# Attention weights as pairs of 16-bit floats, turned by DMA; q and k loaded twice, one copy above the other

## The chip, the core and the metric

The kernel runs on one core of a Trainium2 chip. A core has five engines with queues of their own: TensorE (PE; its weight loads are listed apart as PEld), VectorE (DVE), ScalarE (ACT), GpSimd (POOL) and SyncE (SP), which here issues the DMAs. Each engine works through its own list of instructions in order and waits on semaphores for the others. The metric is the time of one execution in device microseconds; less is better.

## The reference

The kernel computes three layers after one another: block-causal attention, a mixture of experts with dense gates, and a two-layer network with a softmax-weighted activation and a normalization. The change is in the attention alone, cut here to what it computes:

```
B, H, S, D = 4, 8, 576, 64                        # q, k, v: [B, H, S, D] in f32
scores = (1/8) * q @ k^T                          # per (batch, head): 576 x 576
mask   = (row // 64) >= (column // 64)            # blocks of 64
attn   = softmax(where(mask, scores, -1e9))       # divided by (sum + 1e-9)
x      = attn @ v                                 # 2304 x 512 over all heads
...                                               # gates, 8 experts (512 -> 1024 -> 512), then w_in, w_out
```

## The kernel before

The 32 (batch, head) pairs are worked in 16 **head pairs**; the two heads of one are n and n+1. A head's 576 queries are cut into tiles of 128 queries, t = 0 to 3, and the last 64 queries of both heads together are the even head's tile t = 4. So a head pair is nine tiles, and `attention()` works 144 tiles as a software pipeline: in step k it calls `products` for tile k and the later stages for earlier tiles, by the depths in the table `steps` (`("turn", 3)` is tile k - 3).

For one tile the stages are these. `products` forms the scores on PE, in two passes over the split k (`kl`, `kh`) with a q tile that holds the high part in its upper 64 partitions and the low part in the lower 64; `maximum` and `invert` are small DVE operations around ACT's `exponent`, which writes `e` and its row sum. `weight` (L250, POOL) divides `e` by the sum in place. `turn` (L255, L258) transposes each 128 x 128 block of `e` on PE into PSUM. `place` (L278 on ACT, L279 on DVE) splits the turned block into a high and a low fp32r part: ACT copies the high part out of PSUM, DVE subtracts it from the PSUM block. `weigh` (L308, PE) multiplies with the split values `vs`, `sum` (L330, L331) adds the two halves of the result into `xr`, and `split` passes x on to the experts.

`prepare(n)` loads the next head pair: `kraw`, `qraw` and `vraw`, one DMA each, two heads above each other in the 128 partitions. POOL splits k (L64, L159) and v (L64, L184), ACT and DVE split q (L156, L160). `spread` then copies each head's 64 partitions to where the products need them, twice for k: 12 copies of 64 partitions from SBUF to SBUF for each head pair (L169 to L172), all issued on SP.

Into the same list of steps `fill(k)` weaves matmuls of the first expert (gates L405, layers L661 to L699) over the x that is ready; the table `fills` sets how much goes into which steps. The bulk starts at step k = 44. All tiles of PSUM in the attention, scores (`qk`), turned blocks (`tp`, `tq`) and results (`av`), come from one pool of six banks, `psp`. The order within each engine follows the program, moved in places by a scheduler. What comes behind the attention (the gates' normalization, the other experts, the last network) isn't touched.

## Time and profile before

| | |
|---|---|
| time, median of 3 runs | 1886.54 us (1886.08 to 1887.54) |
| the profiled execution | 1884.84 us, span 1883.1 us, granted clock 0.992 |
| PE busy | 1784.1 us (95%) |
| DVE busy | 1385.1 us (74%) |
| POOL busy | 1130.0 us (60%) |
| ACT busy | 852.5 us (45%) |
| DMA | 305.69 MB, mean 162 GB/s |

The span runs from the first to the last instruction; the profiled execution's own time has 1.7 us beside it. The attention with the expert work woven into it takes about the first 380 us. "Busy" is time in which an engine had an instruction of the program under way; the busy time of PE is modelled and counts overlapping matmuls once. The row of POOL's `weight` in the page's list of costly groups is 82.3 us for 144 instructions.

### The profile page before, as it was taken

The numbers are of one execution on the slowest core, as the hardware profiler recorded it, in microseconds if no ns is written. First come the engines' busy times: TensorE is split into PE (matmuls) and PEld (weight loads), VectorE is DVE, ScalarE is ACT, GpSimd is POOL, SyncE is SP. The second block draws the span as 40 slices with busy tenths as digits, with TensorE's granted clock in tenths as the row PEclk, the third lists the DMA queues.
The fourth block names the chain that finished last, engine by engine and source line by source line (L and its number), as shares of the span: only waits on it lengthen the run. The fifth ranks groups of instructions, "written<-read, shape, count | busy, mean of one in ns | idle before, by whom it ended". The sixth has DMA issues, their size and how long they took to land.

```text
span 1883.1 us, 30546 instructions
## 1 busy us (share of the span) xinstructions
PE 1784.1 (95%) x10234; PEld 1161.6 (62%) x10234; DVE 1385.1 (74%) x3199; ACT 852.5 (45%) x1737; POOL 1130.0 (60%) x962
## 2 busy tenths in 40 slices
PE   5799999979999999999999999999999999999999
PEld 4588998868444554554566555665565566566664
DVE  6878777765667666577687878778587898889873
ACT  5666766573777676753422222222322222225332
POOL 7665655345798868672566657668655656582110
PEclk8999999989999999999999999999999999999999
DMA  8665646253667556543656555556555455455433
GB/s 225 165 171 137 165 133 175 66 186 119 223 224 252 183 197 200 160 172 120 205 164 180 171 168 161 159 148 171 167 164 164 148 160 171 148 189 122 107 84 73
DMA packets 227678, 305.69 MB, mean 162 GB/s; under 512 B 57776, under 2 KB 113728, under 8 KB 225600
## 3 DMA queue, kind: packets, MB, share of 16 engines
q1 hardware_dynamic: 227520, 303.73, 54.2%
q8 instruction: 81, 1.33, 0.3%
q14 instruction: 77, 0.63, 0.1%
HBM read 190.86 MB, written 75.05 MB: 141 GB/s over the span
## 4 chain that ended last, share of the span: by engine, by line
PE 51%; POOL 14%; issue 14%; DVE 9%; DMA 5%; ACT 5%; SPq 2%; POOLq 0%; ACTq 0%; DVEq 0%
PE yps L842 4%; PE yps L844 4%; PE yps L843 4%; POOL hf L907 3%; POOL hb L910 3%; POOL w L567 2%; PE av L308 2%; POOL W L567 2%; PE psb L844 2%; PE psb L842 2%; PE psb L843 2%; PE ops L1316 2%; PE ops L1318 2%; PE ops L1317 2%; PE hps L661 1%
## 5 line engine op out<-in xcount | busy, mean ns | idle before, releaser
L907 POOL TENSOR_TENSOR hf<-hb,hf 128x768 f16<-128x768 f32 x196 | 322.3, 1665 | 202.2 <-ACT hf L906 198.6
L843 PEld LDWEIGHTS <-W 128*128 128x128 f16 x1960 | 191.6, 98 | 158.4 <-issue 33.0
L906 ACT CAST hf<-hb 128x768 f16<-128x768 f32 x196 | 155.9, 830 | 275.6 <-DVE hb L910 108.3
L842 PEld LDWEIGHTS <-W 128*128 128x128 f16 x1960 | 191.8, 98 | 135.2 <-ACT W L566 4.7
L844 PEld LDWEIGHTS <-W 128*128 128x128 f16 x1960 | 191.7, 98 | 128.1 <-POOL W L567 1.3
L842 PE MATMUL yps<-hf,W 128*128 128x384 f16 x784 | 255.1, 326 | 3.6 <-DVE acc L954 2.7
L843 PE MATMUL yps<-hf,W 128*128 128x384 f16 x784 | 255.6, 326 | 0.0
L844 PE MATMUL yps<-hf,W 128*128 128x384 f16 x784 | 254.8, 326 | 0.0
L954 DVE SCALAR_TENSOR_TENSOR acc<-yps,rscw,acc 128x384 f32<-128x384 f32 x364 | 215.9, 609 | 20.2 <-PE yps L844 19.1
L842 PE MATMUL psb<-X,W 128*128 128x384 f16 x504 | 164.2, 326 | 13.1 <-DVE u L854 7.5
L844 PE MATMUL psb<-X,W 128*128 128x384 f16 x504 | 164.0, 326 | 0.3 <-POOL W L567 0.3
L843 PE MATMUL psb<-X,W 128*128 128x384 f16 x504 | 164.3, 326 | 0.0
L910 POOL TENSOR_TENSOR hb<-hb 128x768 f32<-128x768 f32 x84 | 153.9, 1832 | 11.0 <-DVE hb L899 7.6
L854 DVE TENSOR_TENSOR u<-psb,r 128x384 f32<-128x384 f32 x168 | 91.3, 552 | 75.0 <-ACT r L868 36.5
L250 POOL TENSOR_SCALAR e<-e,sv 128x128 f32<-128x128 f32 (+2 forms) x144 | 82.3, 574 | 99.7 <-DVE sv L246 32.8
L1001 PE MATMUL yps<-w,h 128*128 128x512 f16 x336 | 127.3, 379 | 6.1 <-DVE h L888 3.3
L567 POOL TENSOR_TENSOR w<-raw,w 128x512 f16<-128x512 f32 (+1 forms) x96 | 122.0, 1289 | 10.8 <-ACT w L566 10.6
L1002 PE MATMUL yps<-w,h 128*128 128x512 f16 x336 | 127.3, 379 | 0.0
L1003 PE MATMUL yps<-w,h 128*128 128x512 f16 x336 | 127.0, 379 | 0.0
L842 PE MATMUL psc<-X,W 128*128 128x384 f16 x336 | 109.5, 326 | 5.7 <-DVE psa L854 2.8
L842 PE MATMUL psa<-X,W 128*128 128x384 f16 x336 | 109.5, 326 | 4.7 <-ACT r L868 4.6
L843 PE MATMUL psa<-X,W 128*128 128x384 f16 x336 | 109.5, 326 | 0.0
(266 smaller groups left out, 4473.4 us busy)
## 6 DMA issues: line engine op xcount, KB each, us to landing
W<-fd SPq DMA_DIRECT2D x392, 256.0 KB, 3.0
fd<-W SPq DMA_DIRECT2D x154, 256.0 KB, 2.1
raw<-in_w1s SPq DMA_DIRECT2D x14, 1024.0 KB, 6.1
raw<-in_w SPq DMA_DIRECT2D x14, 1024.0 KB, 7.5
fd<-w SPq DMA_DIRECT2D x84, 128.0 KB, 2.2
raw<-in_w SPq DMA_DIRECT2D x40, 256.0 KB, 3.3
kh<-khigh SPq DMA_DIRECT2D x64, 144.0 KB, 2.6
kl<-kraw SPq DMA_DIRECT2D x64, 144.0 KB, 2.7
```

What stands on the lines that cost most here:

```text
L567: nc.gpsimd.tensor_tensor(t[:, 1, :], raw, full(t[:, 0, :]), op=ALU.subtract)
L842: nc.tensor.matmul(ps, wh, xl, start=start and kc == 0, stop=False, skip_group_check=True)
L843: nc.tensor.matmul(ps, wh, xh, start=False, stop=False, skip_group_check=True)
L844: nc.tensor.matmul(ps, wl, xh, start=False, stop=stop and kc == 1, skip_group_check=True)
L854: nc.vector.tensor_tensor(to, bank[g, a], tmp[g, "r1" if a == "b" else name[1:]], op=ALU.add)
L906: nc.scalar.copy(hi, a)
L907: nc.gpsimd.tensor_tensor(lo, a, hi, op=ALU.subtract)
L910: eng.tensor_tensor(o, a, b, op=ALU.subtract)
L954: nc.vector.scalar_tensor_tensor(a, ps, r, a, op0=ALU.mult, op1=ALU.add)
L1001: nc.tensor.matmul(ps, hl, ws[c][:, 0, :], start=c == 0, stop=False)
L1002: nc.tensor.matmul(ps, hh, ws[c][:, 1, :], start=False, stop=False)
L1003: nc.tensor.matmul(ps, hh, ws[c][:, 0, :], start=False, stop=c == 3)
```

## The change

What it does, by parts (the line numbers here are those of the changed kernel):

- `weight`, the PE transposes of `turn` and `place` are gone. A new stage `halve`, at depth 2, has ACT write the high 16-bit half of `e` times the reciprocal sum (out of SBUF, `e` now has 640 columns with the last 64 zero), and DVE write the low half by a subtraction whose two tensors are both in SBUF (L284). The new `turn`, at depth 2 too, is a DMA transpose on SP from `eh` into the tiles `a1`, `a2` (L292; two of 64 partitions for tile t = 4, L296).
- The values are scaled by a power of two from their sum of squares and split into 16-bit halves; the scale is found by an ACT square (L192), a matmul with ones (L197) and five small DVE operations, and taken back out in `sum`. `weigh` multiplies 16-bit operands.
- q and k of each head are loaded from DRAM straight into both halves of the partitions, eight DMAs of 64 partitions and one of `vraw` for a head pair; `spread` is gone. k and q are split head by head, so each of these operations runs twice for a head pair.
- Depths: `weigh` from 5 to 6, `sum` from 6 to 7, `split` from 7 to 8. The `a1` and `a2` tiles have four buffers instead of two.

```
     def prepare(n):
...
+        for i in range(2):
+            kr, qr = krs.take(), qrs.take()
+            for r in (slice(0, D), slice(D, P)):
+                nc.sync.dma_start(kr[r], kT[b, h + i])
+            for r in (slice(0, D), slice(D, P)):
+                nc.sync.dma_start(qr[r], qT[b, h + i])
+            raws.append((kr, qr))
+            if i == 0:
+                nc.sync.dma_start(vraw, v[b, h // 2])
+                iv = ivs.take()
...
+        def high(i):
+            pool_copy(kh, kr)
+            nc.scalar.activation(q, qr, AF.Copy, scale=0.125)
+        def low(i):
+            nc.gpsimd.tensor_tensor(kl, kr, r32(kh), op=ALU.subtract)
+            nc.vector.scalar_tensor_tensor(
+                q[D:P], qr[D:P], 0.125, r32(q[D:P]), op0=ALU.mult, op1=ALU.subtract
+            )
...
+            nc.scalar.activation(vjunk, vraw, AF.Square, accum_out=r32(iv[:, 2:3]))
...
+            nc.tensor.matmul(ps[:, 0:1], ones, r32(iv[:, 2:3]), start=True, stop=True)
+            halved(iv[:, 0:1], ps[:, 0:1])
...
-        def spread(i):
-            for r in (slice(0, D), slice(D, P)):
-                nc.sync.dma_start(r32(kh[r]), r32(kh2[half]))
-                nc.sync.dma_start(r32(kl[r]), kraw[half])
-            nc.sync.dma_start(r32(q[0:D]), r32(qh2[half]))
-            nc.sync.dma_start(r32(q[D:P]), qraw[half])
...
-        def weight(self):
-            e = self.e[:, 0 : self.nk]
-            nc.gpsimd.tensor_scalar(e, e, self.rs, 1.0, op0=ALU.mult, op1=ALU.mult)
+        def halve(self):
+            k = self.k = self.t + 1
+            e = self.e[:, 0 : k * P].rearrange("p (k q) -> p k q", q=P)
+            eh = self.eh = ehs.take()
+            hi, lo = (eh[:, 0:k, s, :] for s in range(2))
+            nc.scalar.activation(hi, e, AF.Copy, scale=self.rs)
+            nc.vector.scalar_tensor_tensor(lo, e, self.rs, hi, op0=ALU.mult, op1=ALU.subtract)
 
         def turn(self):
-            self.tp = tp = psp.tile([P, 4, P], F32, tag="ps", name="tp")
-            for kt in range(min(self.t + 1, 4)):
-                nc.tensor.transpose(tp[:, kt, :], self.e[:, kt * P : kt * P + P], ident)
...
-        def place(self):
...
-            for dst, src in work:
-                nc.scalar.copy(dst(0), src)
-                nc.vector.tensor_tensor(dst(1), src, r32(dst(0)), op=ALU.subtract)
+            src = self.eh[:, 0 : self.k].rearrange("p k s q -> p (k s q)")
+            if t < 4:
+                a, c = (parts[n][0], t * P) if t < 2 else (parts[n][1], 64 + t * P - 256)
+                to = a.rearrange("p k s c -> p (k s) c")[:, 0 : 2 * self.k, c : c + P]
+                nc.sync.dma_start(to, src, transpose=True)
+                return
+            for i, c in ((0, 320), (1, 0)):
+                to = parts[n + i][1].rearrange("p k s c -> p (k s) c")[:, :, c : c + D]
+                nc.sync.dma_start(to, src[i * D : i * D + D], transpose=True)
...
         steps = (
-            ("products", 0), ("turn", 3), ("weigh", 5),
-            ("maximum", 0), ("exponent", 1), ("invert", 1), ("weight", 2),
-            ("place", 3), ("sum", 6), ("split", 7), ("prep", 0),
+            ("products", 0), ("weigh", 6),
+            ("maximum", 0), ("exponent", 1), ("invert", 1), ("halve", 2),
+            ("turn", 2), ("sum", 7), ("split", 8), ("prep", 0),
         )
```

How the order of instructions moves, at three places in the middle of the attention. On PE, around the shared tile t = 4 of a head pair, before (`tp` is a turned block, `av` the result):

```order
L219 MATMUL qk<-kl_139,q_133 128x288
L220 MATMUL qk<-kh_136,q_133 128x288
L255 MATMUL tp<-ident,e_147 128x128 x2
L308 MATMUL av<-a_1_130,vs_145 128x320 x8
L308 MATMUL av<-a_1_132,vs_145 128x64 x2
L210 MATMUL qk<-kl_139,q_133 128x256
L211 MATMUL qk<-kh_136,q_133 128x256
```

And now at the same place (`vt` is the sum of squares of the values):

```order
L249 MATMUL qk<-kl_142,q_136 128x288
L250 MATMUL qk<-kh_139,q_136 128x288
L197 MATMUL vt<-iv_149,ones 128x1
L240 MATMUL qk<-kl_142,q_136 128x256
L241 MATMUL qk<-kh_139,q_136 128x256
L326 LDWEIGHTS vs_145
L326 MATMUL av<-a_1_132,vs_145 128x320
```

The transposes are gone, one small matmul has come in before the next head pair's first products, and the weight loads of the 16-bit `weigh` stand as instructions of their own.

On DVE, three tiles' subtractions of `place` before, with what lies between them (`tp` and `tq` are in PSUM):

```order
L279 TENSOR_TENSOR a_1_130<-tp,a_1_130 128x4x2x64
L279 TENSOR_TENSOR a_1_132<-tq,a_1_132 64x128
L279 TENSOR_TENSOR a_1_128<-tp,a_1_128 128x128
L229 TENSOR_REDUCE sv<-qk 128x1
L160 SCALAR_TENSOR_TENSOR qraw<-qraw,qhigh 128x576
L279 TENSOR_TENSOR a_1_128<-tp,a_1_128 128x2x128
```

And now the low halves of `halve` (`e` and `eh` are in SBUF):

```order
L284 SCALAR_TENSOR_TENSOR eh_158<-e_152,sv,eh_158 128x3x128
L259 TENSOR_REDUCE sv<-qk 128x1
L276 RECIPROCAL sv<-sv 128x1
L284 SCALAR_TENSOR_TENSOR eh_154<-e_153,sv,eh_154 128x4x128
L275 TENSOR_SCALAR sv<-sv 128x1
L284 SCALAR_TENSOR_TENSOR eh_155<-e_151,sv,eh_155 128x128
```

The subtraction stands about where it stood, earlier in its tile's life by one step, with both tensors out of SBUF.

On SP, one head pair's copies and loads before:

```order
L170 DMA kl_139<-kraw 64x576
L169 DMA kh_136<-khigh 64x576 x2
L170 DMA kl_139<-kraw 64x576
L171 DMA q_133<-qhigh 64x576
L172 DMA q_133<-qraw 64x576
L147 DMA kraw<-in_kT 128x576
L148 DMA qraw<-in_qT 128x576
L354 DMA xd<-xr_150 128x576
L149 DMA vraw<-in_v 128x640
```

And now, the transposes of one head pair's last tiles with the loads of the next (`kr`, `qr`, `vraw`) between them:

```order
L292 DMA_TRANSPOSE a_3_130<-eh_154 128x2x128
L292 DMA_TRANSPOSE a_3_130<-eh_155 128x4x128
L292 DMA_TRANSPOSE a_3_134<-eh_156 128x6x128
L169 DMA vraw<-in_v 128x640
L164 DMA kr_162<-in_kT 64x576 x2
L166 DMA qr_164<-in_qT 64x576 x2
L292 DMA_TRANSPOSE a_3_134<-eh_157 128x8x128
```

The copies out of `khigh`, `kraw`, `qhigh` and `qraw` are gone, the loads are more, and the transposes of the tiles stand in one list with them.

## Rows read from the trace of the kernel before

**Rows 1.** Stretches: busy us (count) of PE, PEld, DVE, ACT, POOL, clock, DMA share, GB/s.

```profile
0.00:66.80 66.80, 37.01 (x192) 31.70 (x192) 43.11 (x149) 38.42 (x108) 47.72 (x75) 0.87 0.75 200
66.80:99.90 33.10, 25.82 (x161) 20.56 (x162) 29.25 (x112) 24.86 (x79) 22.99 (x37) 1.00 0.68 179
99.90:172.30 72.40, 71.87 (x410) 62.00 (x411) 54.08 (x176) 47.04 (x130) 43.80 (x58) 1.00 0.60 157
172.30:210.40 38.10, 35.92 (x241) 31.75 (x240) 32.88 (x118) 26.61 (x82) 23.56 (x34) 1.00 0.64 165
210.40:364.70 154.30, 151.67 (x932) 138.93 (x932) 111.11 (x363) 97.83 (x275) 83.89 (x114) 1.00 0.47 130
```

**Rows 2.** The same for L356 alone, which DVE runs once a head pair.

```profile
66.80:99.90 33.10, 1.50 (x2) 1.00 0.68 179
99.90:172.30 72.40, 2.17 (x3) 1.00 0.60 157
172.30:210.40 38.10, 1.50 (x2) 1.00 0.64 165
210.40:364.70 154.30, 4.44 (x6) 1.00 0.47 130
```

**Rows 3.** Chain that ended last, 100 to 140 us: start, us, what.

```profile
118.08 1.31 PE av L308 x10
...
123.07 0.44 PE tp L255 x4
```

**Rows 4.** Timeline of PE at 1000 us: start, us, what.

```profile
999.89 0.33 PE L842 MATMUL psc<-X,W 128*128 128x384 f16 x1
1000.05 0.33 PE L843 MATMUL psc<-X,W 128*128 128x384 f16 x1
```

**Rows 5.** Groups by line, 0 to 380.3 us: busy us, mean ns, idle before.

```profile
L279 DVE TENSOR_TENSOR a<-tp,a 128x512 fp32r<-128x512 f32 x48 | 32.8, 683 | 4.3 <-ACT a L278 3.3
...
L245 DVE TENSOR_SCALAR sv<-sv 128x1 f32<-128x1 f32 x144 | 21.2, 148 | 23.1 <-ACT e L236 21.7
...
L279 DVE TENSOR_TENSOR a<-tp,a 128x384 fp32r<-128x384 f32 x32 | 17.5, 546 | 1.3 <-ACT a L278 0.8
...
L279 DVE TENSOR_TENSOR a<-tp,a 128x256 fp32r<-128x256 f32 x32 | 13.4, 418 | 4.8 <-ACT a L278 4.7
...
L160 DVE SCALAR_TENSOR_TENSOR qraw<-qraw,qhigh 128x576 fp32r<-128x576 f32 x16 | 16.9, 1058 | 20.1 <-ACT qhigh L156 20.1
...
L279 DVE TENSOR_TENSOR a<-tp,a 128x128 fp32r<-128x128 f32 x32 | 9.0, 280 | 0.4 <-ACT a L278 0.2
...
L279 DVE TENSOR_TENSOR a<-tq,a 64x128 fp32r<-64x128 f32 x16 | 4.3, 271 | 0.0
```

**Rows 6.** Groups by line, 395 to 450 us, of DVE.

```profile
L726 DVE SCALAR_TENSOR_TENSOR X<-b,sx,X 128x384 f16<-128x384 f32 x12 | 9.6, 800 | 1.1 <-ACT X L725 1.1
```

**Rows 7.** L160 and L726 by themselves: duration min/median/max.

```profile
L160 DVE SCALAR_TENSOR_TENSOR qraw<-qraw,qhigh x16: 739/816/1780, 5.3 to 321.7; 128x576 fp32r<-128x576 f32 x16
...
L726 DVE SCALAR_TENSOR_TENSOR X<-b,sx,X x36: 522/619/1645, 399.9 to 882.9; 128x384 f16<-128x384 f32 x36
```

**Rows 8.** Timelines of DVE and POOL near 128 us.

```profile
127.98 1.73 DVE L160 SCALAR_TENSOR_TENSOR qraw<-qraw,qhigh 128x576 fp32r<-128x576 f32 x1
...
127.66 1.43 POOL L159 TENSOR_TENSOR kraw<-kraw,khigh 128x576 fp32r<-128x576 f32 x1
```

**Rows 9.** Stretches as in the first group, around 1710 us and 30 us.

```profile
1709.40:1712.00 2.60, 2.60 (x12) 2.13 (x12) 2.60 (x5) 1.57 (x3) 0.00 (x0) 1.00 0.75 140
30.00:35.00 5.00, 2.46 (x16) 2.15 (x15) 2.83 (x12) 3.32 (x10) 3.75 (x6) 0.84 1.00 316
```

**Rows 10.** SP: issue of a transpose (L1310) and of a copy (L169), min/median/max.

```profile
L1310 SPq DMA_TRANSPOSE lt<-lh x18: 1232/1245/1363, 1708.4 to 1860.7; - x18
...
L169 SPq DMA_DIRECT2D kh<-khigh x64: 461/587/1226, 5.1 to 334.2; - x64
```

**Rows 11.** Timeline of PE at the start.

```profile
12.95 0.55 PE L210 MATMUL qk<-kl,q 128*128 128x256 f32 x1 [12.95 <-DMA q<-qraw]
```

More of the change, by code (lines that the diff above doesn't have):

```diff
@@ L176, in step2, with step3 @@
+        def step2():
+            high(1)
+            nc.gpsimd.tensor_scalar(vraw, vraw, r32(iv[:, 1:2]), 1.0, op0=ALU.mult, op1=ALU.mult)
+            for i in range(2):
+                pool_copy(heads[n + i][3][:, :, 0:D], vraw[:, i])
+        def step3():
+            low(1)
             for i in range(2):
                 vs = heads[n + i][3]
-                pool_copy(vs[:, :, 0:D], vraw[:, i])
-        def step3():
-            spread(1)
-            for i in range(2):
-                vs = heads[n + i][3]
-                nc.gpsimd.tensor_tensor(vs[:, :, D:P], vraw[:, i], r32(vs[:, :, 0:D]), op=ALU.subtract)
+                nc.gpsimd.tensor_tensor(vs[:, :, D:P], vraw[:, i], vs[:, :, 0:D], op=ALU.subtract)
@@ L198, in __init__ @@
             if t == 0:
-                a24 = parts[n - 1][1:] if n % 2 else (a2s.take(), a4s.take())
-                parts[n] = (a1s.take(), *a24)
+                if n % 2 == 0:
+                    for i in range(2):
+                        parts[n + i] = (a1s.take(), a2s.take())
         def products(self):
@@ L293, in weigh @@
             vs = heads[self.n][3]
-            a1, a2, a4 = parts[self.n]
+            a1, a2 = parts[self.n]
             self.av = av = psp.tile([P, 512], F32, tag="ps", name="av")
             if part == 0:
-                work = [(av[:, 0:256], kt, lambda s, kt=kt: a1[:, s, kt, :]) for kt in range(2)]
+                work = [(av[:, 0:256], kt, lambda s, kt=kt: a1[:, kt, s, :]) for kt in range(2)]
             else:
@@ L460, in total @@
         return ps[:, 0:1]
-    def halved(t, ssq):
-        nc.vector.tensor_single_scalar(t, ssq.bitcast(U32), 24, op=ALU.logical_shift_right)
-    def power(o, t, bound):
-        nc.vector.tensor_scalar(o, t, -1.0, float(bound + 189), op0=ALU.mult, op1=ALU.add)
-        nc.vector.tensor_single_scalar(o, o, 23, op=ALU.logical_shift_left)
     def scale_x():
```

92 lines of the change are left out of this document (43 added, 49 removed).

## The prediction

> **What bounds the kernel now.** I read the table of stretches first, cut where DVE's once-a-head-pair maximum (L356) falls, so that each stretch holds whole head pairs. Its first number is the stretch's length, then the busy time of each engine [rows 1]. The counts of L356 say how many head pairs a stretch has: two from 66.8 us, three from 99.9, two from 172.3, six from 210.4 [rows 2]. Two regimes show. In the nine head pairs of 99.9 to 172.3 and 210.4 to 364.7 us PE is busy 71.87 + 151.67 = 223.5 of 226.7 us, 98.6%: PE is the bound, with expert matmuls between the tiles. DVE is busy there 54.08 + 111.11 = 165.2 us, 73%. In the two pairs of 66.8 to 99.9 us, where hardly any expert work is woven in, PE is busy 78% and DVE 29.25 of 33.1 us, 88%: DVE is nearest to the bound. The two pairs from 172.3 us lie between (PE 35.92, DVE 32.88 of 38.1 us). Behind 380 us nothing is changed, so the forecast is the sum of these stretches, the start and the tail.
>
> **What PE loses.** A head pair has 25 transposes (1+2+3+4+5 blocks in the even head, 1+2+3+4 in the odd). The chain of waits gives 0.44 us for four on PE's path, 0.11 each [rows 3]: 2.75 us a head pair. The value products stream the same columns. Ten of them take 1.31 us for 2560 columns [rows 3]; 16-bit matmuls of 384 columns follow each other every 0.16 us [rows 4], which makes 1.07 us, so the two runs of ten in a head pair give back 2 x 0.24. Against that stands one new 1-column matmul with f32 weights; no row of it is in the attention, and I take one or two transposes' 0.11 us for it. Together PE loses 3.0 us a head pair.
>
> **What DVE loses and gains.** The subtractions of `place` (L279, out of PSUM) sum to 32.8 + 17.5 + 13.4 + 9.0 + 4.3 = 77.0 us, 4.81 us a head pair [rows 5]. The new low half has both tensors in SBUF. Two operations of before are of that kind: q's low part (L160) and the split of x for the later experts (L726), which has the new one's very operands: f32, a scale for each partition, a 16-bit high half. Undisturbed they take 739 ns for 576 columns and 522 ns for 384 [rows 7], that is 1.13 ns a column and 88 ns fixed. A head pair's nine tiles have 3200 columns: 3.62 + 0.79 = 4.41 us, 0.40 less than now. q's low part is now done twice: +0.74. Five small operations for the values' scale, at the 148 ns of L245 [rows 5]: +0.74. Undisturbed that is +1.1 us a head pair.
>
> But they are disturbed. L160 averages 1058 ns against 739 [rows 5, 7] and L726 800 against 522 [rows 6, 7]: 0.32 and 0.28 us more each. One case shows why: the L160 at 127.98 us lasts 1.73 us because POOL's subtraction of k, begun at 127.66, runs until 129.09 [rows 8]; what is left from there, 0.62 us, is near the undisturbed length. Which reads lock each other out is also a rule of the Trainium skill (SBUF — State Buffer, section Who interferes with whom): a DVE instruction with two SBUF inputs contends with a GpSimd instruction that reads SBUF, and the one that comes second waits for the whole other instruction. The rows agree. By that rule alone every new low half can wait, where L279, with one input in PSUM, could not. A head pair will have 11 such operations (nine low halves, two of q) where it has one. How long each waits is bounded below by L726's median, 619 - 522 = 0.10 us [rows 7], above by half of the 0.99 us (1.73 - 0.74) of the case shown, 0.50. I take 0.25, just under L726's mean, since POOL loses `weight` and so is busy somewhat less. So 11 x 0.25 - 0.32 (what L160 waits already) = +2.4, and DVE gains 3.5 us a head pair; 1.9 at the lower end, 6.3 at the upper.
>
> **The stretches after.** Where two engines come out level, neither runs at 98.6%; I take 94%, between PE's share today and the 88% of DVE from 66.8 us.
> - The nine pairs: PE 223.5 - 27.0 = 196.5, DVE 165.2 + 31.5 = 196.7 us; over 0.94 that is 209.3 instead of 226.7: -17.4.
> - The pairs from 172.3 us: DVE 32.88 + 7.0 = 39.9, over 0.94 42.4 instead of 38.1: +4.3.
> - The pairs from 66.8 us: DVE 29.25 + 7.0 = 36.3, over 0.94 38.6 instead of 33.1: +5.5.
> - The first two pairs keep slack (DVE 43.11 of 66.8 us), but they start earlier: the first product waited until 12.95 us for a copy of q [rows 11], and the first L160 started at 5.3 us [rows 7]. Without copies in between about 8 to 9 us: -4.
> - The tail: `sum` and `split` come a step later, at 24 to 26 us for nine steps; +2, the landing of the last transposes with it.
>
> Sum -9.6 us on the profiled 1884.84 us (span 1883.1): 1875.2 us. The median of the runs is 1.7 us above the profiled execution: **1877 us**.
>
> What I cost at nothing, and its cover. ACT: the high halves replace copies of the same size, and even a second q pass and the square at L160's 1.06 us each add some 2 us to 97.83 / 6 = 16.3 us in pairs of 25.7. POOL loses `weight` and gets a second split of k; busy 83.89 of 154.3 us, it has room, and only its locks count. SP: a transpose of 1024 columns holds SP 1.245 us, a copy 0.59 [rows 10]. The 50 blocks of 128 columns that a head pair turns come to 7.8 us if issue goes with the columns, the 12 copies that go were 7.1, and six loads more come in: some 4 us more of SP in 23. If the scheduler's list let a load that waits for POOL stand ahead of due transposes, `weigh` on PE would wait for it, and with it all expert matmuls queued behind.
>
> **The transposes' time** is hidden as long as they land before `weigh`, four steps (some 9 us) after `halve`. From 1709.4 to 1712 us the trace shows two transposes of 256 KB at 140 GB/s with a DMA share of 0.75, that is 187 GB/s of busy time; ordinary traffic near 30 us makes 316 at a share of 1.00 [rows 9]. The 1.64 MB of a head pair are then 8.8 us of all DMA engines. The 12 copies that go (1.77 MB) were 5.6, the doubled loads (0.59 MB more) cost 1.9: net +5.1 us. In the nine pairs the DMA share goes from 12.1 of 25.7 us (0.47) to about 17 of 23; from 66.8 us, from 11.3 (0.68 of 16.55) to 16.4 of 19.3. The Trainium skill says otherwise of the rate (Advanced Engine Details and Errata, section X-Bar Transpose (TRN2)): transposes as fast as ordinary DMAs, 350 to 400 GB/s. By it they would be an estimated 4.4 us and the DMA engines no busier than now; the sum would stay, the third rival below would go. The trace disagrees, so that rival stays.
>
> **Rivals.**
> - *The low halves hardly wait* (0.10 us each, DVE +1.9): PE alone bounds the nine pairs, 196.5 / 0.985 = 199.5 (-27.2), the lighter stretches pay +0.8 and +2.0. With start and tail -26.4: 1860 us. For it speaks the median of L726, which is near its least; against it, means count.
> - *The shared read path decides, and it is slower.* Place: DVE behind POOL's subtractions of k and v, which now come twice as often. At 0.41 us a wait, between L160's mean and the upper bound, DVE gains 5.3 us a head pair: the nine pairs need 212.7 / 0.94 = 226.3, nothing gained; the others pay +8.1 and +9.2. Sum +15: 1901 us. The sign turns at 0.31 us a wait, just L160's mean; that is why I am not sure of it.
> - *Transposes come late.* With the DMA engines 75 to 85% full and one list on SP, `weigh` waits 1.5 us a head pair in 13 pairs beyond the sum: +20, 1897 us. For it speaks the transposes' low rate; against it, four steps of room.
>
> **Chances.** Forecast 0.44 (own range 1864 to 1889), hardly any waits 0.22, shared path 0.18, late transposes 0.16. The range must reach both sides: 1852 to 1900. About 0.2% (3.8 us) is what a measurement of this kernel can tell from no change, 1882.8 to 1890.3. Of the forecast's 0.44, 0.34 lies below that, 0.07 in it and 0.03 above; all but 0.01 of the second case is faster, and of the two slower cases 0.06 falls inside and 0.03 below. Faster 0.58, same 0.14, slower 0.28.
>
> **What would show it.** Right: a head pair in the middle near 23 us; DVE and PE both above 90% there; no L255, and L284 of 640 columns nearer 1.06 us than the undisturbed 0.81 (640 x 1.13 ns + 88), with POOL's L185 or L213 under way when it is long; PE starting near 8 us. Wrong: PE waiting in front of L326 for a DMA (late transposes), DVE idle behind ACT's high half, or ACT waiting on the raw loads; a granted clock of 1.2 instead of 2.4 GHz where PE now has gaps between tiles, as in the first 66.8 us (0.87), would make the lighter stretches longer than I count. Behind 380 us I expect the same durations; a difference there would come from the order alone.

## The result, and the profile after

The changed kernel takes 1901.37 us (median; 1896.43 to 1902.47) where the kernel before took 1886.54 beside it: 1.0074 times as long, 95% interval 1.0056 to 1.0092, some 14 us slower. One execution of the kernel before took 4739.83 us and is left out of the ratio. The forecast was 1877 us, faster; the range ended at 1900. The profiled execution took 1901.56 us, its span is 1899.8 us, 16.7 more than before.

The table of stretches of the changed kernel, cut where DVE's once-a-head-pair maximum (now L377) falls, answers to [rows 1]:

```profile
0.00:73.50 73.50, 35.00 (x146) 26.06 (x146) 59.12 (x175) 48.54 (x122) 49.08 (x69) 0.84 0.72 172
73.50:115.10 41.60, 24.11 (x116) 17.14 (x117) 35.66 (x121) 31.67 (x83) 22.23 (x27) 0.75 0.77 172
115.10:186.10 71.00, 63.34 (x323) 48.30 (x322) 64.60 (x200) 56.33 (x141) 36.68 (x38) 0.95 0.78 170
186.10:233.90 47.80, 39.45 (x240) 31.86 (x239) 43.10 (x134) 35.01 (x93) 23.24 (x25) 1.00 0.69 159
233.90:374.80 140.90, 127.93 (x728) 107.35 (x726) 121.00 (x373) 108.86 (x275) 72.33 (x73) 0.98 0.77 169
```

I call the stretch from 73.5 us "pairs 3 and 4" (head pairs), the one from 186.1 us "pairs 8 and 9", and the two others behind 115.1 us "the nine pairs". Read against [rows 1], DVE's busy time (the third) has grown in every stretch. PE's (the first) has shrunk in all but pairs 8 and 9. Neither fills its stretch: in pairs 3 and 4 DVE is busy 86% and PE 58%, and the granted clock is 0.75 where it was 1.00. The terms of the sum:

| term | forecast, us | measured, us |
|---|---|---|
| first two head pairs | -4 | +6.7 (66.8 to 73.5) |
| two from 66.8 us | +5.5 | +8.5 (33.1 to 41.6) |
| the nine that PE bounded | -17.4 | -14.8 (226.7 to 211.9) |
| two from 172.3 us | +4.3 | +9.7 (38.1 to 47.8) |
| last pair, tail | +2 | -0.8 (to 389.6 us) |
| behind the attention | 0 | +7.4 (1502.8 to 1510.2) |
| sum | -9.6 | +16.7 |

The stretches don't hold the same work, though. They are cut where a line of `split` runs, which now comes a step later, and the expert matmuls are spread over them in another way (counted by their lines in the two traces; idle is the length less PE's busy time):

| stretch | expert matmuls, before and now | PE idle, before and now, us |
|---|---|---|
| first two head pairs | 2, 2 | 29.8, 38.5 |
| pairs 3 and 4 | 6, 6 | 7.3, 17.5 |
| the nine pairs | 641, 572 | 3.2, 20.6 |
| pairs 8 and 9 | 93, 128 | 2.2, 8.3 |

In pairs 8 and 9 the expert matmuls take 24.0 us of PE where they took 15.1, in the nine pairs 11.2 us less than before. So part of the -14.8 and of the +9.7 is work that moved from one stretch to the other; pairs 3 and 4 are the clean comparison.

What PE did in 1899.8 us can be split in three. Its busy time is 1761.7 us. Half of what falls into stretches with a granted clock of 0.5 (1.2 GHz) is the price of the clock, as the same matmuls take twice as long there. The rest of the span is idle. Added up over the trace of each profiled execution:

| kernel | work at the full clock | lost to the clock | idle |
|---|---|---|---|
| before | 1772.4 | 11.7 | 98.9 |
| changed | 1730.4 | 31.4 | 138.0 |

So PE did lose 42 us of work, and 39 us of idle time and 20 us of slow clock took their place (this says what PE did, not what caused it). The longest waits of PE in the attention (who waited for whom, us in total, times, longest):

```profile
PE vt L197 <- ACT vjunk L192: 39.6, 8, 9.1
PE av L326 <- DMA a<-eh: 17.7, 13, 2.6
```

The first is the new 1-column matmul for the values' scale (`vt`); 7.7 us of it is the start. The first products came at 8.11 us instead of 12.95, but then PE stood 9.09 us in front of the second `vt`:

```profile
8.11 0.56 PE L240 MATMUL qk<-kl,q 128*128 128x256 f32 x1
...
21.81 0.59 PE L197 MATMUL vt<-iv,ones 128*128 128x1 f32 x2 [9.09 <-ACT vjunk L192]
```

How such a wait comes about at the loads for the fifth head pair, and what the clock does then, in the timeline (start, us, engine, line, in brackets the idle time before):

```profile
77.75 1.22 SPq L292 DMA_TRANSPOSE a<-eh  x1
...
79.02 0.58 SPq L164 DMA_DIRECT2D kr<-in_kT  x1
...
79.65 1.23 SPq L166 DMA_DIRECT2D qr<-in_qT  x2
...
80.98 0.53 SPq L169 DMA_DIRECT2D vraw<-in_v  x1
...
81.56 1.11 SPq L164 DMA_DIRECT2D kr<-in_kT  x2
...
82.71 1.23 SPq L166 DMA_DIRECT2D qr<-in_qT  x2
...
84.05 6.54 SPq L292 DMA_TRANSPOSE a<-eh  x5
...
84.93 0.74 ACT L192 ACTIVATE vjunk<-vraw 128x640 bf16<-128x640 f32 x1 [0.46 <-DMA vraw<-in_v]
...
85.81 0.58 PE L197 MATMUL vt<-iv,ones 128*128 128x1 f32 x2 [6.32 <-ACT vjunk L192]
...
88.08 2.40 PE L326 MATMUL av<-a,vs 128*128 128x320 f16 x10 [1.05 <-DMA a<-eh]
...
94.06 1.25 PE L326 MATMUL av<-a,vs 128*128 128x320 f16 x10 [0.57 <-DMA a<-eh]
```

SP issues almost without a pause: loads and transposes share one list, the values are issued at 80.98, ACT squares them at 84.93, and PE, whose next products stand behind vt in its list, does nothing for 6.3 us. Five transposes that were due meanwhile go out from 84.05 us on. After the gap ten value products take 2.40 us at 1.2 GHz; at 94.06 us, at the full clock again, 1.25. The gap, what follows it and the time around 94.06 us in the table's form (the granted clock is the third number from the end):

```profile
79.50:85.80 6.30, 0.00 (x0) 0.00 (x0) 5.62 (x17) 5.23 (x14) 2.25 (x2) 0.71 0.83 228
85.80:92.40 6.60, 5.54 (x23) 3.83 (x24) 5.37 (x19) 3.57 (x8) 6.02 (x7) 0.50 0.80 150
...
93.20:99.20 6.00, 2.89 (x19) 1.94 (x17) 5.96 (x24) 5.29 (x14) 0.97 (x2) 1.00 0.57 137
```

DVE is busy 57.3 us more (1442.4 instead of 1385.1), 3.6 us a head pair, as forecast (3.5); the terms behind that sum are not. Groups of the low halves, to be held against [rows 5, 7], and the two lines by themselves (min/median/max ns):

```profile
L186 DVE SCALAR_TENSOR_TENSOR q<-qr,q 64x576 fp32r<-64x576 f32 x32 | 31.5, 985 | 12.3 <-ACT q L180 11.7
...
L284 DVE SCALAR_TENSOR_TENSOR eh<-e,sv,eh 128x640 f16<-128x640 f32 x16 | 16.6, 1040 | 1.6 <-ACT eh L283 1.5
```

```profile
L284 DVE SCALAR_TENSOR_TENSOR eh<-e,sv,eh x144: 332/666/1867, 12.8 to 378.2; 128x128 f16<-128x128 f32 x32, 128x256 f16<-128x256 f32 x32, 128x384 f16<-128x384 f32 x32, 128x512 f16<-128x512 f32 x32
...
L186 DVE SCALAR_TENSOR_TENSOR q<-qr,q x32: 751/756/1862, 6.5 to 343.4; 64x576 fp32r<-64x576 f32 x32
```

All 144 low halves take 105.2 us, 6.58 us a head pair and 0.24 us each above the 4.41 us that I took for undisturbed. But that value was too low. While POOL stood idle from 75.4 to 81.97 us, a low half of 512 columns took 0.73 us and one of 128 columns 0.33, where 1.13 ns a column and 88 ns make 0.67 and 0.23:

```profile
78.14 0.73 DVE L284 SCALAR_TENSOR_TENSOR eh<-e,sv,eh 128x512 f16<-128x512 f32 x1
...
79.40 0.33 DVE L284 SCALAR_TENSOR_TENSOR eh<-e,sv,eh 128x128 f16<-128x128 f32 x1
...
81.97 0.67 POOL L64 TENSOR_SCALAR kh<-kr 128x576 fp32r<-128x576 f32 x1 [6.56 <-DMA kr<-in_kT]
```

The medians of the five shapes, 0.35, 0.47, 0.62, 0.74 and 0.90 us for 128 to 640 columns, make 5.27 us a head pair; measured from them a low half waits about 0.14 us. The longest is again one that met POOL, here the split of an expert's weights:

```profile
274.52 1.87 DVE L284 SCALAR_TENSOR_TENSOR eh<-e,sv,eh 128x640 f16<-128x640 f32 x1
...
274.44 3.08 POOL L579 TENSOR_TENSOR w<-raw,w 128x512 fp32r<-128x512 f32 x2 [1.99 <-ACT w L578]
```

SP's side, to be held against [rows 10]: a transpose costs SP 1.23 us whether it has 256 or 1280 columns.

```profile
L292 SPq DMA_TRANSPOSE a<-eh x128: 1167/1227/2545, 15.6 to 380.9; - x128
...
L296 SPq DMA_TRANSPOSE a<-eh x32: 1205/1232/2653, 22.5 to 373.3; - x32
```

Behind the attention the durations are the same, but the work is more: of the gates' matmuls (L426) 32 stood ahead of its end, before 46, and 60 instead of 64 of each kind of the second layer (L709 to L711). The 7.4 us there are 5.9 of PE's work at the full clock and 3.4 lost to the clock, less 1.9 of idle time.

### The profile page after: what moved, and what is told of

Its sections match the earlier page's. It is cut to its first block, busy times and chain, and to the rows that moved or that the text cites. A ratio compares the mean times of both kernels' runs of the same rounds, so it can differ in the third digit from the quotient of the medians.

```text
span 1899.8 us, 29717 instructions
## 1 busy us (share of the span) xinstructions
PE 1761.7 (93%) x9866; PEld 1111.5 (59%) x9866; DVE 1442.4 (76%) x3279; ACT 897.6 (47%) x1769; POOL 1109.6 (58%) x871
## 3 DMA queue, kind: packets, MB, share of 16 engines
q8 instruction: 78, 1.28, 0.3%
## 5 line engine op out<-in xcount | busy, mean ns | idle before, releaser
L966 DVE SCALAR_TENSOR_TENSOR acc<-yps,rscw,acc 128x384 f32<-128x384 f32 x364 | 215.1, 608 | 18.6 <-PE yps L856 17.5
L854 PE MATMUL psb<-X,W 128*128 128x384 f16 x504 | 164.8, 327 | 12.3 <-DVE u L866 6.2
L284 DVE SCALAR_TENSOR_TENSOR eh<-e,sv,eh 128x128 f16<-128x128 f32 (+2 forms) x144 | 104.1, 731 | 8.5 <-ACT eh L283 7.5
```

Source lines behind the costliest of these rows:

```text
L284: nc.vector.scalar_tensor_tensor(lo, e, self.rs, hi, op0=ALU.mult, op1=ALU.subtract)
L854: nc.tensor.matmul(ps, wh, xl, start=start and kc == 0, stop=False, skip_group_check=True)
L966: nc.vector.scalar_tensor_tensor(a, ps, r, a, op0=ALU.mult, op1=ALU.add)
```

## The experiments

All are timed against the kernel before on the same chip; "+14" means so many us above it by the ratio. Each ratio has its own runs of the kernel before, so two experiments differ clearly only where their intervals lie apart.

| run | ratio (95% interval) | us |
|---|---|---|
| changed kernel | 1.0074 (1.0056 to 1.0092) | +14 |
| vt_late | 1.0122 (1.0100 to 1.0144) | +23 |
| both_heads | 1.0133 (1.0112 to 1.0155) | +25 |
| late_both | 1.0091 (1.0075 to 1.0107) | +17 |
| weigh_8 | 1.0117 (1.0090 to 1.0143) | +22 |
| warm | 1.0101 (1.0084 to 1.0119) | +19 |
| no_scale | 1.0064 (1.0041 to 1.0087) | +12 |
| no_qlow | 1.0028 (1.0016 to 1.0039) | +5 |
| no_ksub | 1.0048 (1.0033 to 1.0063) | +9 |
| no_turn | 1.0012 (1.0002 to 1.0021) | +2 |
| old_load | 1.0357 (1.0336 to 1.0377) | +67 |
| one_load | 1.1420 (1.1391 to 1.1449) | +268 |
| loads_pool | 1.0475 (1.0457 to 1.0493) | +90 |
| pe_turn | 1.0127 (1.0106 to 1.0147) | +24 |
| load_alone | 1.0070 (1.0049 to 1.0091) | +13 |
| load_q | 1.0021 (1.0012 to 1.0031) | +4 |
| load_k | 1.0032 (1.0019 to 1.0046) | +6 |
| load_apart | 1.0068 (1.0053 to 1.0083) | +13 |
| f16_alone | 0.9983 (0.9973 to 0.9993) | -3 |

### The waits on PE

**vt_late.** The matmul for the scale three steps later.

```diff
         def step1():
             low(0)
-            nc.tensor.matmul(ps[:, 0:1], ones, r32(iv[:, 2:3]), start=True, stop=True)
...
         def step3():
             low(1)
+            nc.tensor.matmul(ps[:, 0:1], ones, r32(iv[:, 2:3]), start=True, stop=True)
...
+        def step4():
+            nc.gpsimd.tensor_scalar(vraw, vraw, r32(iv[:, 1:2]), 1.0, op0=ALU.mult, op1=ALU.mult)
...
-                    if work and k % 9 in (3, 4, 5, 7):
+                    if work and k % 9 in (3, 4, 5, 7, 8):
```

> The sum-of-squares matmul of the values (vt) and the five small DVE operations move to the preparation step in which k and q of the odd head get their low parts, three steps later, and POOL's scaling and splitting of v into a step behind it; nothing is left out. Theory A (in the changed kernel PE stands 4.5 to 9 us in front of vt in each of the second to sixth head pairs, 31 us in all, because vt waits for the next pair's loads while products that are ready are queued behind it; SP, 18.5 of 20.8 us busy in a head pair of the light stretch, is why the loads come late): the idle time before vt falls from 31 us to under 6, the four light head pairs before 115 us become 8 to 20 us shorter, 1881 to 1893 us in all. Theory B (DVE with its waits on the shared SBUF path bounds the light stretches, 35.7 of 41.6 us): the idle time only moves to other PE instructions, 1898 to 1903 us.

The wait at vt went (7.6 us are left, the start), and the kernel got slower. PE's waits now:

```profile
PE av L328 <- DMA a<-eh: 58.7, 17, 8.5
PE vt L203 <- ACT vjunk L192: 7.6, 1, 7.6
```

The transposes took vt's place, 58.7 us instead of 17.7. Theory B had the direction (the idle time moves) but not the time, which is above its range; A's gain did not come.

**both_heads.** Five loads instead of nine (an excerpt; q in the same way). The two heads' tiles of k are one buffer now, and those of q another, so each comes free for the next loads only as a whole.

```diff
-            for r in (slice(0, D), slice(D, P)):
-                nc.sync.dma_start(kr[r], kT[b, h + i])
+            for r in (slice(0, D), slice(D, P)):
+                nc.sync.dma_start(kr[r], kT[b, h : h + 2].rearrange("h d s -> d h s"))
...
```

> The loads of both heads go in one DMA for each half of the partitions: four DMAs of 64 partitions x 2 x 576 and one of the values, instead of nine; the source rows are read in the same way, nothing is left out. SP issues 2.4 us less of its 18.5 us a head pair, and a transpose that stands behind the loads waits 3 us instead of 5.5. Theory A (SP's one list delays the transposes: from the end of the low half to the start of the issue 3.2 us on average, up to 9.3): the attention ends 4 to 10 us earlier than in the changed kernel, 1891 to 1897 us. Theory B (DVE, 86 to 90% busy in the light stretches): within 2 us, 1899 to 1903. Theory C (the DMA engines, 0.77 busy, take the transposes slowly): the bytes are the same, so 1899 to 1903 too.

Slower, by none of the theories. SP did get room: from the end of a tile's low half to the start of its transpose 0.5 to 1.1 us pass on average in each stretch (2.4 to 3.0 in the changed kernel up to the last pair). But PE still waited 29.2 us for transposes. So more room on SP alone doesn't shorten the kernel, at least not with these buffers.

**late_both.** Both edits together.

> The edits of two earlier runs together: vt and the values' scaling later, and the loads of both heads in one DMA each; nothing is left out. Theory E (three near-full stages take turns: without vt's wait PE waited 58.7 us for transposes, with prompt transposes it waited for vt and the loads): with both waits gone the light pairs fall to what DVE allows, pairs 3 and 4 38 to 39.5 us, 1884 to 1895 us. If DVE alone bounds them already: within 4 us of the two single runs, 1901 to 1911.

Not to be told from the changed kernel (the intervals overlap); pairs 3 and 4 take 41.4 us. Theory E fell too: PE is idle 140.0 us in all, now for transposes (19.0), for ACT's exponent (17.9), for vt (13.0) and in smaller waits. So neither wait went in full, and no run took both away.

**weigh_8.** Two more steps between the transposes and the value products (an excerpt; `sum`, `split` and the expert work move with it, there are six value tiles, and the square of the values writes into one of them).

```diff
-            ("products", 0), ("weigh", 6),
+            ("products", 0), ("weigh", 8),
...
```

> The value products come two steps later in the pipeline (weigh at 8, sum 9, split 10), with six instead of four value tiles and the expert work starting two steps later; nothing is left out. The transposes get some 4.6 us more room, 13.8 instead of 9.2 us, against their 12 to 13 us at worst. If the transposes are late but SP keeps up in the mean (theory A, lateness): the PE waits in front of the value products and the clock's low stretches go, the attention ends 8 to 15 us earlier, some of it given back by the later end of the pipeline: 1888 to 1896 us. If SP or DVE is full (throughput): within 3 us, plus up to 5 for the longer tail, 1899 to 1906 us.

No gain, though PE waits only 0.8 us for transposes now; it waits 42.1 us for ACT in front of vt, and 8.9 for DVE. Room for late transposes by itself is not what is missing. The run with vt later and `weigh` at depth 8 together, which would have taken away both waits, wasn't made.

**no_scale.** No square, no vt, no small DVE operations, no scaling of v.

```diff
...
-                nc.scalar.activation(x, av[...], AF.Copy, scale=iv[olo : olo + D])
+                nc.scalar.activation(x, av[...], AF.Copy, scale=2.0**-15)
...
```

> Leaves out finding the values' scale: no square on ACT, no vt matmul, none of the five small DVE operations, no scaling of v on POOL; the constant power of two of the weights is taken out in sum. All else as in the changed kernel. If the scale's part costs what the run with transposes on PE suggests (9.7 us over the loads alone, PE standing in front of vt): 1886 to 1893 us. If the transposes only take over vt's place as what PE waits for, as in the run with vt later: 1897 to 1902 us.

Some 2 us better, within the intervals, as the second reading had it: PE waits 38.2 us for transposes instead of 17.7 and is idle 146.2 us in all. DVE is busy 15.7 us less and POOL 13.6. Leaving out the scale alone does not give the loss back.

**warm.** Unused matmuls, to keep PE busy.

```diff
+                for _ in range(10 if n < 10 else 0):
+                    nc.tensor.matmul(s[:, 0:P], ident16, ident16, start=True, stop=True)
...
```

> Adds work that nothing uses: in the first five head pairs ten 16-bit matmuls of 128 columns on PE ahead of each score tile's products, 100 a head pair, some 5.5 us of PE at the full clock; they overwrite a bank that the products then start anew, the result is unchanged. Theory D (PE's granted clock of 1.2 GHz, 0.70 to 0.82 of full between 25 and 115 us, lengthens the chain: ten value products take 2.4 us there against 1.25): the clock between 25 and 115 us rises above 0.95 and the first four pairs end 6 to 12 us before the 115.1 us of the changed kernel, 1889 to 1896 us. If the low clock costs nothing because DVE or the transposes bound these pairs: the same end or up to 5 us later, 1900 to 1907 us.

The clock rose only from 0.75 to 0.84 in pairs 3 and 4 (75% of them PE-busy now), and they took 43.9 us instead of 41.6. The run does not give theory D the clock it asks for, so it neither shows nor refutes that price.

### DVE and the shared path

**no_qlow.** q's low halves left out.

> Leaves out DVE's subtraction for the low part of q (two of 0.985 us a head pair), so the scores are formed from a wrong low part; all else stays. Theory B (DVE bounds the light stretches): pairs 3 and 4 and pairs 8 and 9 each 3 to 4 us shorter, the first two 3, the rest 5: 1886 to 1891 us. Theories A and C (SP or the DMA engines delay the transposes): within 3 us, 1898 to 1902.

DVE is busy 32.3 us less (1442.4 to 1410.1) and the time is 9 us less, about as theory B had it. But pairs 3 and 4 lost 0.5 us of their 41.6, while pairs 8 and 9 lost 6.7: B is right in the sum and wrong in the place.

**no_ksub.** POOL's subtractions left out.

```diff
-            nc.gpsimd.tensor_tensor(kl, kr, r32(kh), op=ALU.subtract)
...
-                nc.gpsimd.tensor_tensor(vs[:, :, D:P], vraw[:, i], vs[:, :, 0:D], op=ALU.subtract)
```

> On the changed kernel, leaves out POOL's subtractions for the low parts of k and of the values (their low parts are constant zeros), the POOL operations that a DVE operation with two SBUF inputs was seen to wait for; all else stays. If DVE's waits on POOL are a part of the loss: the low halves of the weights fall from 0.73 us on average to near their undisturbed 0.5, q's from 0.985 to 0.76, DVE loses some 35 us, and as leaving out q's low parts did (30 us of DVE, 11 us of time) the kernel takes 1886 to 1892 us. If the waits are hidden behind the transposes: 1897 to 1902 us.

The low halves fell to 0.637 us on average (q's to 0.829), so the meetings with POOL are real:

```profile
L284 DVE SCALAR_TENSOR_TENSOR eh<-e,sv,eh 128x128 f16<-128x128 f32 (+2 forms) x144 | 90.5, 637 | 14.4 <-ACT eh L283 13.3
...
L189 DVE SCALAR_TENSOR_TENSOR q<-qr,q 64x576 fp32r<-64x576 f32 x32 | 26.5, 829 | 18.8 <-ACT q L184 18.3
```

DVE is busy 21.3 us less and POOL 78.3; the time is 5 us less, between the two expectations, and the interval still touches that of the changed kernel. By both runs a microsecond of DVE is worth about a quarter of one in time (9 / 32.3 and 5 / 21.3); no_scale gives less (2 / 15.7), within its interval. By a quarter the 57.3 us that DVE gained with the change are some 14 us. This is an estimate, and it leaves out what the work that PE lost should have given back.

### The transposes and the DMA side

**no_turn.** No DMA transposes.

```diff
-            ("turn", 2), ("sum", 7), ("split", 8), ("prep", 0),
+            ("sum", 7), ("split", 8), ("prep", 0),
...
```

> Leaves out the DMA transposes: the value products read constant tiles of zeros, so the attention's output is zero; all other work stays, halves included. SP loses its ten transposes, 12.5 of 18.5 us a head pair, and the DMA engines 1.6 MB. Theory A (SP full, loads late): vt's waits go, the two head pairs before 115 us take 36 to 38 us instead of 41.6, and PE's 18 us of waits for transposes go: 1870 to 1885 us. Theory B (DVE): DVE's work is what it was, 1895 to 1902 us.

12 us better than the changed kernel, between the two expectations; as the attention's output is zero, what follows works on other data. The stretches up to the fourteenth head pair after the first, as above:

```profile
0.00:68.70 68.70, 35.56 (x144) 25.88 (x144) 58.09 (x170) 46.36 (x116) 47.47 (x62) 0.72 0.50 141
68.70:107.90 39.20, 26.58 (x112) 17.54 (x112) 36.46 (x122) 30.47 (x81) 21.35 (x24) 0.76 0.32 95
...
179.80:217.70 37.90, 33.21 (x204) 27.16 (x205) 36.62 (x125) 29.71 (x80) 19.96 (x22) 0.95 0.36 105
217.70:351.00 133.30, 124.90 (x726) 106.14 (x723) 123.80 (x384) 107.50 (x277) 70.15 (x70) 0.99 0.30 90
```

Here DVE fills 93 to 97% of the middle stretches, which is what I had forecast for the change: pairs 3 and 4 take 39.2 us (38.6 forecast). The attention ends at 363.0 us, 26.6 earlier, but what follows takes 1523.0 us instead of 1510.2: 3.0 us of that are work left over (of each kind of the second layer 49 or 50 matmuls stood ahead of the end instead of 60), 7.7 are lost to the clock. The run also frees PE of every wait for ACT's and DVE's halves, so it bounds the price of the turn, it does not measure the DMA engines alone.

**old_load.** The loading part undone in the changed kernel.

> Undoes the loading part alone: q and k loaded once for two heads, split once, and spread by twelve SBUF copies as in the kernel before; the 16-bit weights, their DMA transposes and the scaled values stay. SP then has 12 copies at 0.57 us and 3 loads against 9 loads at 0.6 us, 2 to 3 us more a head pair, so 21 of the 20.8 us of a light head pair. Theory A (SP full): the light stretches get longer still, 1903 to 1925 us. Theory B (DVE with POOL on the shared path): POOL subtracts k once a pair instead of twice and DVE q once, some 1.5 us a pair less of DVE, 1885 to 1896 us.

Far worse than either theory. SP issues 45.4 us of the 49.5 of pairs 3 and 4 (37.1 of 41.6 in the changed kernel), the DMA engines are busy 0.87, and PE waits 15.0 us for spread q. Beside the transposes the twelve copies nearly fill SP and the DMA engines; the run doesn't tell the two apart.

**one_load** and **loads_pool.** The same loads as one DMA with a repeated source, and from another queue.

```diff
-                nc.sync.dma_start(kr[r], kT[b, h + i])
...
+            nc.sync.dma_start(kr, kT[b, h + i][None].to_broadcast([2, D, S]))
...
```

> Each head's k and q are loaded by one DMA of 128 partitions that reads the same 64 rows twice, instead of two DMAs of 64 partitions; bytes and everything else as in the changed kernel. SP issues five loads a head pair instead of nine, some 2.4 us less of its 18.5. Theory A (SP's list makes the loads late): vt waits 2 us less in each of five head pairs, 1891 to 1898 us. Theory B (DVE): within 2 us of the changed kernel, 1899 to 1903.

```diff
-                nc.sync.dma_start(kr[r], kT[b, h + i])
+                nc.gpsimd.dma_start(kr[r], kT[b, h + i])
...
```

> The nine loads of a head pair are issued from GpSimd's queue instead of SP's; the same bytes, nothing left out. SP then has the transposes and x's copies alone, 13 us of 20.8. Theory A (SP's list): the transposes start within 1 us of their halves, the attention ends 10 to 20 us earlier, 1884 to 1893 us, unless issuing costs POOL more than its idle half. Theory C (DMA engines): they are as busy as before, the transposes land as late, 1899 to 1903 us. Theory B (DVE): 1899 to 1905.

Both miss, for reasons of their own, so neither tests the theories. The repeated source made the loads themselves slow (below). Issued by GpSimd, a load takes 0.54 us of POOL, which then stands in one list with k's split: vt waits 51.3 us on PE, transposes 67.4.

```profile
L166 POOL DMA_DIRECT2D qr<-in_qT x64 | 35.0, 548 | 27.4 <-ACT q L180 10.8 <-DVE sv L275 4.6 <-DVE q L186 3.7
L164 POOL DMA_DIRECT2D kr<-in_kT x64 | 34.0, 536 | 1.3 <-POOL kl L185 0.9
```

### The parts by themselves

**load_alone.** On the kernel before, with the `prepare` of the changed one less the scale.

> The loading part alone on the kernel before: q and k of each head loaded twice, one above the other, and split head by head; weights, transposes and values as before. If loading twice is a gain (twelve SBUF copies and 1.2 MB of DMA traffic go, PE starts 4 to 5 us earlier): 1879 to 1885 us. If the second split of k and q on POOL and DVE eats it up: 1886 to 1892 us.

The loading part by itself loses 13 us, above both expectations, where I had forecast a gain at the start. Its stretches and q's low halves:

```profile
0.00:70.50 70.50, 41.65 (x192) 34.98 (x192) 50.06 (x151) 39.31 (x111) 56.13 (x83) 0.81 0.48 142
70.50:107.00 36.50, 26.99 (x160) 22.29 (x160) 32.88 (x112) 26.05 (x82) 28.49 (x42) 0.93 0.32 99
```

```profile
L171 DVE SCALAR_TENSOR_TENSOR q<-qr,q 64x576 fp32r<-64x576 f32 x32 | 44.7, 1398 | 6.2 <-ACT q L165 5.3
```

The DMA engines fell from 0.68 to 0.32 in pairs 3 and 4, and it helped nothing. DVE is busy 32.1 us more and POOL 40.4: q's low half now takes 1.40 us on average; it is called beside k's subtraction for the same head, and 27 of the 32 ran beside one. PE's work at the full clock (1768.4 us) and its idle time (97.9) are those of before; 32.8 instead of 11.7 us are lost to the clock. So in this profile the whole loss is PE at 1.2 GHz, half of it behind the attention.

**load_q, load_k.** One half of it each.

> On the kernel before, only q is loaded twice and split head by head (a second pass on ACT and on DVE a head pair); k is loaded, split and spread as before. If DVE's second low half of q, with its waits, is what the doubled loads cost (DVE 2.1 us more a head pair in the run with both, 33 us in all): 1889 to 1896 us. If POOL's second split of k is: 1880 to 1886 us, PE starting earlier.

> On the kernel before, only k is loaded twice and split head by head (a second pass of two operations on POOL a head pair); q is loaded, split and spread as before. If POOL's second split is what the doubled loads cost (POOL 2.5 us more a head pair, PE waiting 22 instead of 16 us for POOL's division, longer waits of DVE on the shared path): 1890 to 1897 us. If DVE's second pass over q is: 1881 to 1886 us.

+4 and +6 us, each in the range of its own theory: both halves cost, and together (13) not clearly more than their sum. q's low half takes 0.87 us where only q is doubled, 1.40 where both are; whether that meeting costs time is what the next run was for.

**load_apart.** DVE's low half of q a step later.

```diff
         def step2():
+            low_q(0)
             high(1)
...
+        def step4():
+            low_q(1)
```

> The loading part alone on the kernel before, as in an earlier run, but DVE's low half of q stands a preparation step later than POOL's subtraction of k for the same head, where both were called one behind the other; the same work. If it is their meeting that costs (q's low half took 1.40 us on average there, 0.74 undisturbed, 19 us of DVE in 32): its mean falls below 1.0 us and the time to 1886 to 1892 us. If the doubled work itself costs it: 1895 to 1900 us.

Undecided: the mean fell only to 1.29 us, as 26 of the 32 still ran beside a subtraction of k on POOL, and the time stayed.

**pe_turn.** Division, transposes and split as before the change, into 16-bit floats; loads and scale as changed.

```diff
-            ("turn", 2), ("sum", 7), ("split", 8), ("prep", 0),
+            ("weight", 2), ("turn", 3), ("place", 3), ("weigh", 5), ("sum", 6), ("split", 7), ("prep", 0),
...
```

> Undoes the low halves in SBUF and the DMA transposes alone: POOL divides, PE transposes, ACT and DVE split out of PSUM as in the kernel before, but into 16-bit floats; the doubled loads, the scaled values and the 16-bit value products stay, with the depths of before. If the turn by DMA with what it needs is the loss: PE gets 25 transposes back, the two light stretches and the start come back to the kernel before or below it, PE's nine pairs gain the 0.48 us of 16-bit value products each: 1874 to 1885 us. If the loads or the scale of the values are the loss (vt's wait on PE, q's second low half on DVE): 1888 to 1900 us.

Slower than the changed kernel, against both expectations: on top of the loads and the scale, low halves in SBUF and the turn by DMA, with their depths and buffers, are worth 10 us.

**f16_alone.** The 16-bit part on the kernel before.

> The 16-bit part alone on the kernel before: loads, spread, POOL's division and PE's transposes as before, the split out of PSUM into 16-bit floats, 16-bit value products; the values are split into 16-bit floats without a scale. If 16-bit value products save PE what I forecast (0.24 us for each ten, 0.48 a head pair): 1877 to 1883 us. If they run no faster than before at these widths (1.25 us for ten against 1.31, as the changed kernel's trace has it): 1882 to 1888 us.

A gain, and the only version that beats both kernels: 1881.32 us. The time alone, 3 us below the kernel before, doesn't separate the two expectations; the durations do. At the full clock a run of ten value products takes 1.28 us on average where the f32 ones take 1.51 (27 such groups in each trace), and PE's work at the full clock falls by 8.0 us, 0.50 a head pair (0.48 forecast). Not all of that reached the time: in this profile 11.2 us more than before went to the slow clock. Two rows of the timelines, single groups of this kernel and of before:

```profile
241.19 1.25 PE L322 MATMUL av<-a,vs 128*128 128x320 f16 x10
```

```profile
245.00 1.43 PE L308 MATMUL av<-a,vs 128*128 128x320 f32 x10
```

## Why the prediction was wrong

**Right.** PE loses 42 us of work in 16 head pairs (forecast 48). The DMA engines are busy 0.77 of 20.8 us in pairs 3 and 4, 16.0 us a head pair (16.4), of which no_turn takes away 9.7 (8.8). The Trainium skill's rate for transposes (Advanced Engine Details and Errata, section X-Bar Transpose (TRN2)) isn't borne out here: 1.64 MB in 9.7 us of DMA engine time are 169 GB/s. L255 is gone, and the first product starts at 8.11 us.

**Right in the sum, by luck in the parts.** DVE gains 3.6 us a head pair (3.5). But the undisturbed low halves take 5.27 us a head pair and not 4.41, for the fit through the shortest durations of two other operations gave 88 ns of fixed time where the new ones have some 0.2 us; the waits are about 0.14 us for a low half and 0.23 for one of q (985 - 756 ns), not 0.25 for each; and the addition in `sum` (L350, 477 ns for its commonest shape where L331 took 421), which I had left out, adds 0.3. Ten value products were read as 1.31 us from the chain, which shows only a part of them; they take 1.51, now 1.28, and the difference comes to nearly the forecast's 0.24. The nine pairs are 14.8 us shorter (17.4), at 23.5 us each, but 11.2 us of expert work left them; PE is busy 90% there and DVE 88%, where the prediction wanted both above 90%.

**The step that failed** is the one from busy times to lengths: "Where two engines come out level, neither runs at 98.6%; I take 94%". It was taken for two engines, with the transposes hidden and SP at "some 4 us more". In pairs 3 and 4, where as few expert matmuls run as before, DVE's busy time came out as forecast (35.7 us, forecast 36.3), but the stretch took 41.6 us and not 38.6: DVE filled 86% and not 94%. SP was busy 89% there (37.1 us) and ACT 76%. Pairs 8 and 9 took 47.8 us and not 42.4, with DVE at 43.1 us instead of 39.9 and at 90%; more expert work is part of that. Without the transposes DVE filled 93% and 97% of these two stretches, so 94% is a fair number for one full engine, and it is the transposes, with the waits and the list on SP that come with them, that took it away here. Taking one of the waits away moved the idle time to another (vt_late, both_heads, late_both, weigh_8, no_scale). Of the variants of the changed kernel two were clearly shorter than it, and both leave work out, on DVE (no_qlow) or on SP and the DMA engines (no_turn). That several nearly full lists in a chain hold each other up is my reading of these runs; no run shows it by itself.

**Four terms were mis-sized with it.** "The first two pairs keep slack ... -4": +6.7, for DVE went from 43.1 to 59.1 us there, and PE, which did start 5 us earlier, soon stood 9.09 us in front of vt. I had priced that matmul at 0.11 us and not asked what is queued behind it; the two matmuls that it became took 0.59 us there, so the wait counts and not the matmul. The tail's +2: the later `split` moves the end of the first stretch, by a step of some 2.3 us (41.6 us in pairs 3 and 4 are 18 steps), and not the tail, which came out at -0.8. "Behind 380 us I expect the same durations": the same durations, but +7.4 us, as matmuls that had run ahead of the attention's end now come behind it, and as 3.4 us more go to the slow clock. And SP: "7.8 us if issue goes with the columns" is ten transposes at 1.23 us, 12.3 and more; SP gained 10.3 us a head pair, not 4. both_heads gave some of that back on SP and got no shorter.

**Named and not priced:** a load that stands ahead of due transposes in SP's list, which the timeline shows at 79 to 84 us, and the granted clock. PE's lost time at 1.2 GHz is 20 us more than before, more than the kernel's whole loss. In the case shown the clock fell in a gap of 6.3 us on PE (0.71 over the gap) and was 0.50 in the 6.6 us behind it. Whether the light stretches would be shorter at the full clock stays open, as warm did not reach it. Between 25 and 115 us of the changed kernel DVE was busy 88% of the time at the full clock and 84% of the time at the slow one, a small difference.

**The rivals.** The shared read path gave 1901 us as its time, and 1901 was measured, but that is luck: it asked for 0.41 us a wait, and DVE gained 3.6 us a head pair, not its 5.3. Late transposes are not the loss by themselves (weigh_8), and stand as a price: no_turn puts some 12 us on the turn with all that it ties together. Hardly waiting low halves had nearly the right wait (0.10 us, about 0.14 measured) and still fall: DVE gained 3.6 us a head pair and not 1.9, and the time went the other way.

**Open.** What a part costs depends on the parts around it: the loads are +13 us alone, scale and 16-bit products +11 on top of them with PE transposes, the turn by DMA -10 again, 16-bit products without a scale -3. By subtraction the scale would cost 14 us in pe_turn; left out of the changed kernel it gives back 2. So the 14 us of the whole change have no single cause that a run shows. Why the doubled loads cost so much clock behind the attention (15.9 against 4.9 us, one profile each) isn't settled.

## What to carry to other kernels

Price a change by what it does to each list, then ask how many lists are nearly full in the same stretch: here the fullest engine reached 93 to 97% of its stretch without the transposes and 86 to 91% with them, and removing one wait did not help. Check that two stretches hold the same work before you compare their lengths. Take an undisturbed duration from a row in which the other engine stood idle, not from the shortest of many. For each new instruction on an in-order engine, however short, write down what stands behind it and what it waits for. And time the parts separately: here one of them was by itself a gain of 3 us.

## What the hardware showed beside that

A load whose source is named twice by a leading step of zero ran two packets at a time: in one_load the packets of 2,304 bytes (a row of k or q, and of x) had exactly two under way for 358 of some 406 us, while in the changed kernel 16 at once was the commonest number. The Trainium skill has this rule (DMA: Bandwidth & Descriptors, section Rules for kernel authors): a leading zero-stride broadcast of c copies confines a DMA to at most c engines. The trace agrees, with c = 2. In that run PE waited 176.5 us for transposes in the attention, 17.7 in the changed kernel.

Issuing a DMA transpose cost SP 1.17 us at least, for 256 columns as for 1280; a plain load of 64 rows 0.47 us at least.
